# The first rows of a fused layer-norm, gated MLP and long-convolution training step: gate and up products of rows 0 and 1 advanced together, weight piece by weight piece

## The chip, the cores and the metric

The kernel runs on one core of a Trainium2 chip. The metric is the device time of one execution in microseconds. Before the change the median of three runs is 1850.38 us (1850.25 to 1850.51). Engines are named as in the profile: PE is the matrix engine, PEld its weight loads, DVE the vector engine, ACT the scalar engine, POOL the general engine and SP the engine that issues most of the transfers; "SPq" or "ACTq" marks an instruction of an engine's sequencer, such as a transfer being issued.

## The reference, cut to what matters

The program computes a forward pass and the gradients of all inputs. For this change only the forward's start matters: a layer norm of x, and two products of the normalised rows with weight matrices.

```python
def _layernorm(x, axis=-1, eps=1e-5):
    m = jnp.mean(x, axis=axis, keepdims=True)
    v = jnp.var(x, axis=axis, keepdims=True)
    return (x - m) / jnp.sqrt(v + eps)
...
        gate = jnp.einsum("bsd,df->bsf", x, W_gate)
        up = jnp.einsum("bsd,df->bsf", x, W_up)
        gate = gate * (lambda x, dt: x.astype(dt))(gate > 0, gate.dtype)
        h = gate * up
        return jnp.einsum("bsf,fd->bsd", h, W_down)
...
    xn = _layernorm(x, axis=-1)
    return x + _A_ref(xn, A_k, A_v, A_shift_k, A_ssm_k, A_ssm_D) + _B_ref(xn, B_W_gate, B_W_up, B_W_down)
```

x has 2048 rows of 1024 bfloat16 values; W_gate and W_up are 1024 by 3584, W_down is 3584 by 1024. The outputs are the result and nine gradients.

## The kernel before

Rows are taken in 16 tiles of 128 rows, columns of the MLP in 7 blocks of 512. `hidden` goes over two halves of eight row tiles, and in each over the seven blocks. For a row tile and a block it makes a gate product and an up product (eight matmuls each over the 1024 inner values, in `gemm8`, line 1111, into the PSUM tiles `ps_g` and `ps_u`), and a product of the incoming gradient tile with the transposed W_down block (`grad_row`, PSUM tile `ps_h`). [...]

A matmul needs the row tile with its inner index on the partitions. For tiles 0 to 5 `flip_xn` makes that on PE: eight 128 by 128 transposes into a PSUM tile `pst_x` (line 1154), then a copy to `xnT` (line 1159) by DVE, for tile 4 by ACT. Tiles 6 and 7 are turned by a transposing transfer.

The layer norm is a Python generator, `layer_norm`; each `next(ln)` emits one stage. Tile 0's mean and variance come from DVE's statistics instructions (line 1016); tile 1's from ACT, which sums a row of 1024 (line 962, `sums`) and then sums the squares after the mean is known. A row's reciprocal root comes from `root` and `inverse`: a few DVE instructions on one or two columns with one ACT square root between them. Tiles 0 and 1 are turned when they are only centred ("bare" rows): the factor `rstd` is put in later, in the relu on ACT (line 1230) and in the product with the mask on DVE (line 1244). Tile 2 and all later tiles are scaled before they are turned. `LN_CHUNKS` says how many tiles are loaded and normalised together: tiles 0 to 3 singly, from tile 4 on by pairs. A pair shares one root. `ln_load` loads a chunk into one of five buffers of four rows each, so the sixth load waits for the first buffer.

The order of the opening is written out by hand in `first_rows`: gate of row 0 (with the transposes of tile 1 after its sixth matmul), gate of row 1, up of row 0, up of row 1 (tile 2 turned after its fifth matmul), gate 2, up 2 (tile 3 turned after its fourth), gate 3, up 3. Before it, `warm` runs 42 small matmuls on zeros. After it come gradient rows 0 and 1; in row 1, after the fourth matmul, `flip_ahead` turns tiles 4 and 5. `chunk` emits stages of the layer norm behind the last ACT instruction of the layer norm.

A scheduler orders each engine's instructions by a priority that grows with the place in the program, and by when it expects their operands. An instruction given to `keep_in_program_order` (in the generator `hold`; through `pri.pin` with `always=True` elsewhere) keeps its place among those so marked. Engines then run their queues strictly in order. Transfers from SP share one queue: x tile 0 (half), the four pieces of the first W_gate block (256 KB each), four of W_up with the load of tile 2 in their middle, tile 3, four transposing loads of W_down with tiles 4 and 5 in their middle, gradient tiles 0 and 1 (transposing), tiles 6 and 7, gradient tiles 2 and 3. The second half of tile 0 and tile 1 are issued by ACT. Stores of the normalised rows go out from POOL: tile 0's at once, those of the other first-half tiles are kept in a list and sent in two groups.

Of the kernel before, what the change touches and what calls it, by code (L numbers as in the profile page):

```python
# [879 lines left out]
class LnMlp:  # L880
# [60 lines left out]
    def ln_load(self, x, xpool, i):  # L941
        if i >= len(self.LN_CHUNKS):
            return
        st0, n = sum(self.LN_CHUNKS[:i]), self.LN_CHUNKS[i]
        xt = xpool.tile([P, 4, self.D], BF16, name="ln_x", tag="lnx")
        rows = x[st0 * P:(st0 + n) * P, :].rearrange("(t p) d -> p t d", p=P)
        sy, ac, h = self.nc.sync, self.nc.scalar, self.D // 2
        parts = {0: ((sy, 0, h), (ac, h, self.D)), 1: ((ac, 0, self.D),)}.get(i, ((sy, 0, self.D),))
        for queue, lo, hi in parts:
            ins = queue.dma_start(out=xt[:, 0:n, lo:hi], in_=rows[:, :, lo:hi])  # L950
            if queue is ac:
                self.tc.keep_in_program_order(ins)
        self.ln_x.append(xt)

    def layer_norm(self, xn_d, jpool, jtag, spool):
# [19 lines left out]
        def root(sm, smb, n, pin, quarter):  # L975
            pin(V.tensor_scalar(out=smb[:, 2, 0:n], in0=smb[:, 1, 0:n], scalar1=LN_EPS, scalar2=None, op0=ALU.add))
            pin(act(sm[:, 4, 0:n], smb[:, 2, 0:n], ACT.Sqrt, scale=0.25))
            if quarter is None:
                pin(act(sm[:, 5, 0:n], smb[:, 2, 0:n], ACT.Copy, scale=0.25))
            else:  # L980
                quarter(V.tensor_scalar(out=sm[:, 5, 0:n], in0=smb[:, 2, 0:n], scalar1=0.25, scalar2=None, op0=ALU.mult))

        def inverse(sm, smb, n, st0, pin, amid=None):
            pin(V.reciprocal(out=sm[:, 6, 0:n], in_=sm[:, 4, 0:n]))
            if amid is not None:
                amid()
            if n == 1:
                ins = V.scalar_tensor_tensor(out=smb[:, 3, 0:n], in0=sm[:, 6, 0:n], scalar=sm[:, 5, 0:n],
                                             in1=sm[:, 4, 0:n], op0=ALU.mult, op1=ALU.add)
                if amid is not None:  # L990
                    pin(ins)
            else:
                V.tensor_tensor(out=sm[:, 5, 0:n], in0=sm[:, 5, 0:n], in1=sm[:, 6, 0:n], op=ALU.mult)
                V.tensor_tensor(out=smb[:, 3, 0:n], in0=sm[:, 4, 0:n], in1=sm[:, 5, 0:n], op=ALU.add)
            self.ln_dve = V.reciprocal(out=self.rstd[:, st0:st0 + n], in_=smb[:, 3, 0:n])
# [11 lines left out]

        h = D // 2
        x0, x1, c1 = self.ln_x[0][:, 0, :], self.ln_x[1][:, 0, :], self.ln_x[1][:, 1, :]
        (s0, b0), (s1, b1) = small(), small()  # L1010
        self.pri.now()

        def stats(x, smb):
            bn = spool.tile([P, 2, 6], F32, name="ln_bn")
            for k in range(2):
                hold(V.bn_stats(out=bn[:, k], in_=x[:, k * h:k * h + h]))  # L1016
                if k == 0:
                    yield
            hold(V.bn_aggr(out=smb[:, 0:2, 0], in_=bn[:].rearrange("p h s -> p (h s)")))

        for _ in stats(x0, b0):
            pass
        def less(c):
            hold(V.tensor_scalar(out=x0[:, c:c + h], in0=x0[:, c:c + h], scalar1=b0[:, 0, 0:1], scalar2=None,
                                 op0=ALU.subtract))

        hold(sums(s1[:, 0, 0:1], x1, ACT.Copy, scale=-1.0 / D))
        hold(act(b1[:, 0, 0:1], s1[:, 0, 0:1], ACT.Copy))
        root(s0, b0, 1, hold, None)
        less(0)  # L1030
        less(h)
        hold(sums(s1[:, 2, 0:1], x1, ACT.Square, bias=b1[:, 0, 0:1]))
        self.xn.append(x0)
        yield
        hold(V.tensor_scalar(out=c1, in0=x1, scalar1=b1[:, 0, 0:1], scalar2=None, op0=ALU.add))
        inverse(s0, b0, 1, 0, hold, lambda: None)
        hold(self.ln_dve)
        self.xn.append(c1)
        yield
        self.pri.now()  # L1040
        hold(V.tensor_scalar(out=b1[:, 1, 0:1], in0=s1[:, 2, 0:1], scalar1=1.0 / D, scalar2=None, op0=ALU.mult))
        root(s1, b1, 1, hold, hold)
        n0 = self.ln_x[0][:, 1, :]
        hold(V.tensor_scalar(out=n0, in0=x0, scalar1=self.rstd[:, 0:1], scalar2=None, op0=ALU.mult))
        nc.gpsimd.dma_start(out=xn_d[0:P, :], in_=n0)
        inverse(s1, b1, 1, 1, hold, lambda: None)
        hold(self.ln_dve)
        yield
        st0 = 2
        for i, n in list(enumerate(self.LN_CHUNKS))[2:]:  # L1050
# [3 lines left out]
            pin, d = hold if n == 1 else free, n // 2 * 2  # L1054

            def centre(j):
                return V.tensor_scalar(out=xt[:, d + j, :], in0=xt[:, j, :], scalar1=smb[:, 0, j:j + 1], scalar2=None,
                                       op0=ALU.subtract if i == 2 else ALU.add)
            if i == 2:
                yield from stats(xt[:, 0, :], smb)  # L1060
            else:
# [4 lines left out]
                if i == 4:  # L1066
                    yield
                ins = V.tensor_scalar(out=smb[:, 0, 0:n], in0=sm[:, 0, 0:n], scalar1=-1.0 / D, scalar2=None, op0=ALU.mult)
# [861 lines left out]
```

## Time and profile before

| what | value |
|---|---|
| median of three runs | 1850.38 us (1850.25 to 1850.51) |
| the profiled execution's own time | 1850.71 us |
| its span, first to last instruction | 1848.9 us |
| PE busy | 1829.2 us, 99% of the span |
| DVE busy | 1118.2 us, 60% |
| ACT busy | 643.9 us, 35% |
| share of the chain that ended last on PE | 98% |
| first transposes of tile 0 | 5.58 us |
| first matmul of gradient row 0 | 22.50 us |
| transposes of tiles 4 and 5 | from 25.15 us |

A line of the timeline gives the start, the length, the engine, the line of the program, the operation, the tile written and read, the shapes, how many were merged, and in brackets the idle time before it with what ended it. Matmuls are pipelined: one of 128 by 512 is listed with 0.38 us, but in a dense run they start 0.216 us apart. A line of the stretches gives the length of a stretch, the busy time and instruction count of each engine in it, the granted PE clock, the share of the transfer engines and the rate.

### The profile page before, as it was taken

What the parts mean: (1) busy time and instruction counts of PE and PEld (TensorE: products, weight loads), DVE (VectorE), ACT (ScalarE), POOL (GpSimd) and SP (SyncE); (2) the same over time, 40 slices, a digit from 0 to 9 for tenths busy, and PEclk for the clock granted to TensorE, in tenths of its full rate; (3) what the DMA queues carried; (4) which work ended last, traced back from release to release, by engine and by line L of the source; (5) the groups of instructions that cost most, each with busy time, mean ns of one, the idle gap of its engine ahead of it and who ended that gap; (6) DMA issues with size and microseconds to landing.
All of it is one profiled execution on the core that took longest, in us unless ns stands there. A gap on an engine that the chain in (4) does not pass through costs nothing.

```text
span 1848.9 us, 32175 instructions
## 1 busy us (share of the span) xinstructions
PE 1829.2 (99%) x12974; PEld 848.1 (46%) x13186; DVE 1118.2 (60%) x1649; ACT 643.9 (35%) x1209; POOL 34.8 (2%) x72
## 2 busy tenths in 40 slices
PE   9999999999999999999999999999999999999999
PEld 5444444444444444444444444444444544444444
DVE  6756898698789758585685667721122222566652
ACT  5644544545444454544544454320000000111100
POOL 2200000000000000000000000000000000000000
PEclk9999999999999999999999999999999999999999
DMA  9997669969767856639567445389999857799963
GB/s 259 282 224 177 156 169 235 217 161 205 187 152 205 240 159 162 169 103 270 130 158 170 142 117 160 106 243 251 219 233 266 198 143 172 171 211 214 208 148 74
DMA packets 746805, 345.18 MB, mean 187 GB/s; under 512 B 578088, under 2 KB 715296, under 8 KB 746656
## 3 DMA queue, kind: packets, MB, share of 16 engines
q1 hardware_dynamic: 732992, 311.39, 70.9%
q10 hardware_dynamic: 9504, 17.04, 3.0%
q0 software_dynamic: 4160, 14.68, 2.3%
q8 instruction: 103, 1.69, 0.4%
q14 instruction: 46, 0.38, 0.1%
HBM read 143.79 MB, written 103.83 MB: 134 GB/s over the span
## 4 chain that ended last, share of the span: by engine, by line
PE 98%; issue 1%; DVE 0%; ACT 0%; ACTq 0%
PE ps_x L1780 21%; PE ps_w L1483 20%; PE ps_h L1111 10%; PE ps_u L1111 10%; PE ps_o L1648 10%; PE ps_g L1111 10%; PE ps_d L1483 9%; PE ps_c L83 4%; PE ps_d L1499 1%; PE ps_w L1499 1%; PE ps_r L1682 0%; PE ps_warm L1170 0%; ACT ln_j L962 0%; PE pst_x L1154 0%; DVE ln_bn L1016 0%
## 5 line engine op out<-in xcount | busy, mean ns | idle before, releaser
L1483 PE MATMUL ps_w<-ugs,xn_nat 128*128 128x512 bf16 x1675 | 375.2, 379 | 4.7 <-issue 2.9
L87 ACT CAST arena<-ps_c 128x512 bf16<-128x512 f32 x576 | 293.8, 613 | 104.6 <-PE ps_c L83 104.3
L1111 PEld LDWEIGHTS <-xnT 128*128 128x128 bf16 x1792 | 171.8, 98 | 208.7 <-issue 5.1
L1483 PEld LDWEIGHTS <-xn_nat 128*128 128x128 bf16 x1728 | 165.3, 98 | 200.8 <-issue 6.1
L343 DVE STREAM_TRANSPOSE arena<-arena 128x1024 f32<-128x1024 f32 x96 | 179.4, 1934 | 112.2 <-ACT arena L87 101.8
L1111 PE MATMUL ps_u<-wu,xnT 128*128 128x512 bf16 x878 | 204.7, 379 | 1.2
L1111 PE MATMUL ps_g<-wg,xnT 128*128 128x512 bf16 x865 | 203.1, 379 | 1.5
L1111 PE MATMUL ps_h<-wdT,goT 128*128 128x512 bf16 x870 | 201.8, 379 | 1.3
L1780 PE MATMUL ps_x<-wuT,guT 128*128 128x512 bf16 x878 | 197.5, 379 | 1.0
L1780 PE MATMUL ps_x<-wgT,ggT 128*128 128x512 bf16 x878 | 197.3, 379 | 0.9
L1798 ACT ACTIVATE w<-xn,m 128x512 f32<-128x512 bf16 x32 | 24.3, 807 | 480.2 <-DVE m L1791 366.8
L1648 PE MATMUL ps_o<-wd,hT 128*128 128x512 bf16 (+1 forms) x879 | 186.7, 372 | 0.9
L1483 PE MATMUL ps_d<-g_nat,hs 128*128 128x512 bf16 x743 | 166.5, 379 | 2.6 <-issue 1.9
L1780 PEld LDWEIGHTS <-guT 128*128 128x128 bf16 x896 | 87.7, 98 | 105.7
L1780 PEld LDWEIGHTS <-ggT 128*128 128x128 bf16 x896 | 87.7, 98 | 105.5
L1111 PEld LDWEIGHTS <-goT 128*128 128x128 bf16 x896 | 86.6, 98 | 104.3 <-issue 1.0
L1648 PEld LDWEIGHTS <-hT 128*128 128x128 bf16 x896 | 87.7, 98 | 100.0
L1378 ACT CAST gh<-ps_h 128x512 bf16<-128x512 f32 x112 | 66.3, 592 | 190.6 <-PE ps_h L1111 181.7
L1486 ACT CAST wi<-ps_w 128x512 bf16<-128x512 f32 x108 | 64.5, 598 | 187.1 <-PE ps_w L1483 151.2
L1640 DVE TENSOR_TENSOR ya<-ya,xe 128x1024 bf16<-128x1024 bf16 x16 | 11.1, 692 | 182.1 <-DMA xe<-xn_d 182.1
L91 DVE TENSOR_TENSOR t<-arena 128x2048 bf16<-128x2048 bf16 x96 | 113.9, 1219 | 0.4
L1483 PEld LDWEIGHTS <-hs 128*128 128x128 bf16 x768 | 73.3, 98 | 88.3 <-issue 1.8
(150 smaller groups left out, 1412.8 us busy)
## 6 DMA issues: line engine op xcount, KB each, us to landing
ugs<-ug_d SPq DMA_DIRECT2D x112, 256.0 KB, 5.2
ug_d<-ru SPq DMA_DIRECT2D x104, 256.0 KB, 3.5
wg<-in_B_W_gate_dram SPq DMA_DIRECT2D x56, 256.0 KB, 4.9
wu<-in_B_W_up_dram SPq DMA_DIRECT2D x56, 256.0 KB, 4.3
hs<-h_d SPq DMA_DIRECT2D x56, 256.0 KB, 4.6
out_dram<-wi SPq DMA_DIRECT2D x56, 256.0 KB, 4.2
h_d<-ht SPq DMA_DIRECT2D x104, 128.0 KB, 2.2
gt<-in_grad_out_dram SPq DMA_DIRECT2D x32, 256.0 KB, 5.5
```

The costliest lines, as they stand in the source:

```text
L83: self.pri.pin(self.nc.tensor.matmul(out, lhsT=lhsT, rhs=rhs, start=start, stop=stop))
L87: self.pri.pin(self.nc.scalar.copy(out=out, in_=in_))
L91: self.pri.pin(self.nc.vector.tensor_tensor(out=out, in0=in0, in1=in1, op=op))
L343: self.pri.pin(self.nc.vector.transpose(out=df[:, c0:c0 + 32, :], in_=sf[:, c0:c0 + 32, :]))
L1111: self.pri.pin(self.nc.tensor.matmul(ps[:], lhsT=xT[:, kt * P:(kt + 1) * P], rhs=w(kt), start=(kt == 0), stop=(kt == self.DT - 1)), always ...
L1378: self.pri.pin(nc.scalar.copy(out=gh[:], in_=ps[:]))
L1483: self.pri.pin(self.nc.tensor.matmul(ps[:], lhsT=lhsT(st), rhs=rhs(st), start=(st == 0), stop=(st == self.ST - 1)))
L1486: self.pri.pin(self.nc.scalar.copy(out=out, in_=ps[:]))
L1499: self.pri.pin(self.nc.tensor.matmul(ps[i][:], lhsT=lhsT(i, st), rhs=rhs(i, st), start=(st == 0), stop=(st == self.ST - 1)))
L1648: nc.tensor.matmul(ps, lhsT=hT[:, kt, :], rhs=self.wd[:, kt, oc], start=(kt == 0), stop=(kt == self.FT - 1))
L1780: nc.tensor.matmul(ps, lhsT=T[:, kt, :], rhs=W[:, kt, oc], start=(i == 0), stop=(i == n - 1))
L1798: nc.scalar.activation(out=w[:, oc], in_=xn[:, oc], func=ACT.Identity, scale=m[:, 7:8], bias=m[:, 6:7])
```

## The change

- Loads: tile 1 moves from ACT's queue to SP's, the first W_gate piece from SP's to ACT's. The load of tile 2 is issued ahead of the second W_up piece, that of tile 3 ahead of the fourth. Tile 5 is no longer loaded with tile 4 but by itself, between gradient tiles 0 and 1 (`ln_rest`). The loads of the gradient tiles and of tiles 6 and 7 are pinned to program order.
- Layer norm: tile 0's mean comes half from a statistics instruction on DVE and half from an ACT sum (`half_mean`); its variance from an ACT square. Tiles 0 and 1 share one root. Tile 2 is also turned when only centred. Tile 3's mean is taken like tile 0's, and tiles 2 and 3 share one root. Tiles 4 and 5 keep one root for both, but each has its own stage of sums and squares.
- Order: 40 warm matmuls instead of 42. Tile 0 is transposed in pieces of 2, 2 and 4. `pair` writes two PSUM banks side by side: gate of row 0 takes weight piece 0, then tile 1 is turned, then pieces 1 and 2 for row 0, pieces 0, 1, 2 for row 1, piece 3 for both. The up rows alternate by weight piece; tile 2 is turned after the sixth pair of matmuls. The mask products of rows 0 and 1 on DVE come together, after tile 3 is turned.
- Stores: those of tiles 0, 1 and 2 are made from separate scaled copies and kept; the groups have four and four stores instead of three and four.

```diff
-        parts = {0: ((sy, 0, h), (ac, h, self.D)), 1: ((ac, 0, self.D),)}.get(i, ((sy, 0, self.D),))
+        parts = ((sy, 0, h), (ac, h, self.D)) if i == 0 else ((sy, 0, self.D),)
+        m = 1 if i == 4 else n
...
+        if i == 4:
+            self.ln_rest = lambda: sy.dma_start(out=xt[:, 1:2, :], in_=rows[:, 1:2, :])
...
+        def half_mean(x, s, b, k):
+            part = spool.tile([P, 2, 6], F32, name="ln_bn")
+            hold(V.bn_stats(out=part[:, 0], in_=x[:, 0:h]))
+            hold(sums(s[:, 0, k:k + 1], x[:, h:D], ACT.Copy, scale=-1.0 / D))
+            hold(V.tensor_tensor(out=s[:, 1, k:k + 1], in0=part[:, 0, 1:2], in1=part[:, 0, 4:5], op=ALU.add))
+            hold(V.scalar_tensor_tensor(out=b[:, 0, k:k + 1], in0=s[:, 1, k:k + 1], scalar=-0.25, in1=s[:, 0, k:k + 1],
+                                        op0=ALU.mult, op1=ALU.add))
...
+            if i == 4:
+                for j in range(n):
+                    hold(sums(sm[:, 0, j:j + 1], xt[:, j, :], ACT.Copy, scale=-1.0 / D))
+                    hold(act(smb[:, 0, j:j + 1], sm[:, 0, j:j + 1], ACT.Copy))
+                    hold(sums(sm[:, 2, j:j + 1], xt[:, j, :], ACT.Square, bias=smb[:, 0, j:j + 1]))
+                    moved(xt[:, n + j, :], xt[:, j, :], smb[:, 0, j:j + 1])
+                    yield
...
-        h = self.DT // 2 if st < 3 else self.DT
-        for k0 in range(0, self.DT, h):
+        k1 = 0
+        for h in {0: (2, 2, 4), 1: (4, 4)}.get(st, (8,)):
+            k0, k1 = k1, k1 + h
...
-        return st < 2
+        return st < 3
...
+                ps = pair("ps_g", wg, ((0, 0), (0, 1), (0, 2), (1, 0), (1, 1), (1, 2), (0, 3), (1, 3)), {0: second_tile})
+                for s in range(2):
+                    gate(s, True, ps=ps[s])
+                    yield from step()
                 next(ln)
...
+                ps = pair("ps_u", wu, [(s, q) for q in range(4) for s in range(2)], {5: third_tile})
+                for s in range(2):
+                    up(s, None, {}, lambda *fs: held.extend(fs), True, ps[s])
+                    yield from step()
+                gate(2, True)
                 yield from step()
                 up(2, None, {3: last_mid})
                 chunk(1)
                 yield from step()
                 gate(3, True)
+                chunk(1)
                 yield from step()
                 up(3, hold=True)
+                chunk(1)
                 yield from step()
...
-                self.warm(42)
+                self.warm(40)
...
-                        for put in self.kept[0:3] if sp == 2 else self.kept[3:7]:
+                        for put in self.kept[0:4] if sp == 2 else self.kept[4:8]:
...
+    first = [b.col_block(B_W_gate, 0, "wg", 0, ahead=tc.nc.scalar)]
     b.first_root()
-    first = [b.col_block(B_W_gate, 0, "wg", 0)]
-    first.append(b.col_block(B_W_up, 0, "wu", 1, lambda: load(2)))
-    load(3)
+    first.append(b.col_block(B_W_up, 0, "wu", 1, {1: lambda: load(2), 3: lambda: load(3)}))
     first.append(b.row_block_T(B_W_down, 0, "wdT", 2, lambda: load(4)))
-    goT = [b.load_T(g, i, "goT", 8 + i) for i in range(2)]
+    goT = [b.load_T(g, 0, "goT", 8, True)]
+    b.ln_rest()
+    goT.append(b.load_T(g, 1, "goT", 9, True))
     load(5)
-    goT += [b.load_T(g, i, "goT", 8 + i) for i in range(2, 4)]
+    goT += [b.load_T(g, i, "goT", 8 + i, True) for i in range(2, 4)]
```

More of the change, by code (lines that the diff above doesn't have):

```diff
@@ L1011, in layer_norm @@
+        c0, c1, n1, n0 = self.ln_x[0][:, 1, :], *(self.ln_x[1][:, k, :] for k in (1, 2, 3))
+        c2, n2 = (self.ln_x[2][:, k, :] for k in (1, 2))
+        (sm, smb), (s2, b2) = small(), small()
         self.pri.now()
[L1013 to L1019, printed above, removed]
@@ L1042, in layer_norm @@
[L1042 to L1047, printed above, removed]
-        yield
-        st0 = 2
-        for i, n in list(enumerate(self.LN_CHUNKS))[2:]:
+        variance(sm, smb, 2, hold)
+        root(sm, smb, 2, hold)
+        inverse(sm, smb, 2, 0, held)
```

198 lines of the change are left out of this document (97 added, 101 removed).

## The prediction

> **What bounds the kernel now.** I read the page first: how busy the matrix engine (PE) is, and the chain that ended last.
>
> ```profile
> span 1848.9 us, 32175 instructions
> PE 1829.2 (99%) x12974; PEld 848.1 (46%) x13186; DVE 1118.2 (60%) x1649; ACT 643.9 (35%) x1209; POOL 34.8 (2%) x72
> PE 98%; issue 1%; DVE 0%; ACT 0%; ACTq 0%
> ```
>
> PE is the bound, and the chain leaves other engines under 2% of the span. The change touches only the opening, so I read that as busy time by stretch, next.
>
> ```profile
> core 0: us, PE busy (x) PEld busy (x) DVE busy (x) ACT busy (x) POOL busy (x), PEclk, DMA share, GB/s
> 5.50:10.60 5.10, 5.05 (x34) 2.73 (x33) 4.16 (x19) 3.45 (x9) 0.32 (x1) 1.00 1.07 357
> 10.60:22.50 11.90, 11.57 (x65) 5.42 (x65) 10.39 (x32) 8.61 (x16) 0.94 (x2) 1.00 1.12 226
> 22.50:26.30 3.80, 3.75 (x30) 2.11 (x30) 3.49 (x13) 1.80 (x5) 1.07 (x2) 1.00 1.08 252
> 26.30:60.00 33.70, 33.54 (x154) 15.23 (x157) 21.77 (x67) 17.86 (x31) 16.10 (x26) 1.00 1.11 271
> ```
>
> PE is idle by only 0.05, 0.33 and 0.05 us up to 26.3 us, and VectorE (DVE) is nearly as full (10.39 of 11.90 us). So what can be won is about one microsecond in 1850; what can be lost is whatever wait the new order makes. Last I read the timeline of the opening for the rows that decide it.
>
> ```profile
> 1.02 4.66 PE L1170 MATMUL ps_warm<-warm 128*128 128x128 bf16 x42 [1.02 <-DVE warm L1167]
> 5.58 1.03 PE L1154 MATMUL pst_x<-ident,ln_x 128*128 128x128 bf16 x8
> 12.42 0.58 SPq L950 DMA_DIRECT2D ln_x<-in_A_q_dram  x1
> 13.84 0.62 PE L1154 MATMUL pst_x<-ident,ln_x 128*128 128x128 bf16 x8 [0.26 <-DVE ln_x L998]
> 17.58 2.66 SPq L1135 DMA_TRANSPOSE goT<-in_grad_out_dram  x2
> 17.73 1.06 ACT L962 ACTIVATE ln_j<-ln_x 128x1024 bf16<-128x1024 bf16 x1 [0.26 <-DMA ln_x<-in_A_q_dram]
> 20.43 0.44 SPq L950 DMA_DIRECT2D ln_x<-in_A_q_dram  x1
> 21.31 1.13 ACT L962 ACTIVATE ln_j<-ln_x,ln_b 128x1024 bf16<-128x1024 bf16 x1
> 22.57 0.17 DVE L1076 TENSOR_SCALAR ln_b<-ln_s 128x2 bf16<-128x2 f32 x1 [0.53 <-ACT ln_j L962]
> 24.51 0.97 DVE L998 TENSOR_SCALAR ln_x<-ln_x,rstd 128x1024 bf16<-128x1024 bf16 x2
> 25.15 1.07 PE L1154 MATMUL pst_x<-ident,ln_x 128*128 128x128 bf16 x16
> ```
>
> See two places. At 13.84 us tile 2's transposes waited for its full normalisation; start to start that gap is 0.63 us where the pitch is 0.216, so 0.42 us is lost (the other visible gap, at 18.63, loses 0.18). At 25.15 us the transposes of tiles 4 and 5 start right behind a chain: load (issued at 12.42), two sums and two squares on ScalarE (ACT), roots, scaling. That chain and PE finish together today; PE loses 0.06 us there.
>
> **The change, part by part.** Starts are those of single instructions in the timeline; landings are the last semaphore update of a transfer.
>
> *Start.* Two warm matmuls go: 2 x 0.107 us. Tile 0's mean takes one half by DVE statistics (0.70) and one by an ACT sum (1 element 0.19, 1024 elements 1.06, so about 0.62 for 512), then 0.16 and 0.22 on DVE, in place of two statistics, an aggregate (0.21) and an addition. The halves landed at 3.51 and 3.70, so the first centred half is done near 5.07 (before: 5.52). PE ends its 40 warm matmuls at 5.27 and starts there, 0.31 us earlier than 5.58. Eight transposes at 0.107 end at 6.12; the copy of the first two (0.29) ends at 6.02, so the first gate matmul starts at 6.12 (before 6.57).
>
> *Tile 1 is turned after two gate matmuls instead of six.* These end near 6.9. Centring of tile 1 needs its load, an ACT sum and mean (5.77 to 7.16 today) and 0.49 us of DVE. Today tile 1's load landed at 5.75 and the transposes could have begun at 7.73; PE came at 7.96, so nobody waited. The load moves to the SP queue and weight piece 0 takes its place on ACT's. If tile 1 lands by 5.2, DVE's copies of tile 0 set it (centring 6.71 to 7.19, turn at 7.25); if as today, 7.73. I take the middle, 7.5: PE idles 0.6 us (ends 0.35 and 0.85) where it did not. Then 8 transposes at 0.056 and 14 matmuls at 0.216 end at 10.97 (10.7 to 11.2); before, 10.60. Landings of weight pieces (6.74, 7.49, 8.23) are all earlier than their matmuls.
>
> *From the up rows to the first gradient row*: 48 matmuls x 0.216 + 16 transposes x 0.056 = 11.26 us, against 11.90 before. Tile 2's turn no longer needs the root (centred near 12.3, wanted at 13.5); up pieces 1 and 3 move back one place each behind the loads of tiles 2 and 3 (from 9.72 to about 10.4, from 11.88 to 12.6, wanted 11.9 and 14.0); tile 3's centring, joint root and scaling end near 16.9, wanted at 17.4. Each is covered, the last by only 0.5 us. Rows 0 and 1, and 2 and 3, share one root: about ten small DVE operations of 0.15 to 0.22 go, tile 3's half statistics and row 2's flag (0.70 and 0.28) come; DVE is about 1 us lighter. The first gradient row would start at 22.2 (22.0 to 22.5; before 22.50). After 12 matmuls (2.59) PE wants tile 4 at 24.8, 0.35 us earlier than now.
>
> *Stores and pins.* Tile 0's store leaves POOL at 10.28 (0.71) and goes to the group at 43 us, where POOL issues four (0.65 each) instead of three, behind nothing on PE: nothing. If that cover went, a later load into the buffer would wait 0.65. It also frees 256 KB of transfer at 13.5 to 14.5 us (0.7 us). The pins on the gradient tiles and on the load of tiles 6 and 7 keep today's order; gradient tile 2 landed at 26.86, wanted at 33.99: nothing.
>
> *Tiles 4 and 5, the term that decides.* One load of 512 KB issued at 12.42 becomes 256 KB there (tile 4) and 256 KB behind gradient tile 0 (tile 5). Its two ACT phases can't end before the second half lands, and the root is joint for both rows. Today: landing 17.65, squares end 22.53, transposes 25.15. When does the second half land? SP's second transposed load behind a plain one stays in issue until that one lands (14.33 to 17.54 behind 17.65; 22.20 to 25.25 behind 25.36). With half the bytes and no store beside it, tile 4 lands near 16.3; gradient tile 0 is then issued 16.3 to 17.6, the new load at 17.7. A plain load amid transposed ones lands late: the one for tiles 6 and 7 landed 5.1 us after the issue ahead of it ended (20.24 to 25.36) for 512 KB, so some 4.1 for half: 21.7. By bytes alone (gradient tile 0's landing 21.41, less 1.4 saved by the store and the smaller load, plus 0.72) it is 20.7; with nothing saved before it, 18.89 + 4.1 = 23.0. I take 21.5, nearest to the like load. From there ACT needs a sum with mean 1.3 and a square 1.25: squares end at 24.1 instead of 22.53. Behind them on ACT's in-order queue waits row 3's relu, and for it row 3's mask and product on DVE. From the squares to the transposes took 2.6 us, some 0.5 of it behind two products: 2.1 alone, or 2.95 if row 3's mask and product (0.66 + 0.34), now traced ahead of the inverse, run first. So tile 4 is turned at 26.2 to 27.05, against 25.15: **1.05 to 1.9 us later**; I take 1.5. The 0.35 us that PE came earlier is spent waiting. With 20.7 the least is +0.25, with 23.0 the most +3.4. Behind 26 us no row shows idle PE to win it back.
>
> The sum: span 1848.9 + 1.5 = 1850.4. The profiled execution took 1850.71 against a median of 1850.38, so its 1852.2 is 1851.9 beside the median.
>
> [...]
>
> **The rivals.** *The second half is in time.* If SP runs further ahead than I think and it lands by about 19.5, squares end at 22.1 and PE takes tile 4 when it comes, at 24.6 to 25.1: 0 to 0.6 us won, 1849.9 likely (1849.6 to 1850.4). For it: SP issued transposes in 1.3 us when unblocked, DMA has idle stretches near 12 us. Against: no plain load issued between transposes landed in under 4 us.
>
> *The wait stretches*: the h_d stores that POOL starts at 21.7, now some 2 us earlier, share the DMA with the new load and it lands past 23, while DVE runs all its products first: +3.4 to +4, 1854.1.
>
> *The clock falls (the far side, slower by over 0.2%).* PE would idle from 24.8 to 26.7 in one piece, longer than any gap now (0.63). If that lost the full clock, the opening shows the price: transposes cost 1.03 us for eight, later 0.61, and the slow state lasted from 1.02 to 6.6 us; 5.6 us at half pace cost 2.8. With the wait, +4.3 to +5: 1855. It decides from the length of idleness at which the clock is taken back, which no gap here shows. [...]
>
> **How the numbers follow.** Forecast 62% (its own range 1850.6 to 1853.7), in time 26%, stretched 6%, clock 6%. Time 1851.9. The range leaves out the clock, half of the stretched case and few of the in-time one: 1849.7 to 1853.7. A measurement here can tell about 0.2%, or 3.7 us, from no change: 1846.7 to 1854.1. No case gains that; the clock and a little of the stretched case lose it: faster 0.01, same 0.92, slower 0.07.
>
> **What would show it.** Right: first transposes near 5.27 and a PE gap before tile 1's near 7.5; no gap at tile 2's; the first gradient row at 22.0 to 22.5; then one gap of 1.5 to 2 us before tile 4's transposes, ended by DVE's scaling, with ACT waiting for tile 5's load until near 21.5. Wrong: that load landed before 20, a gap elsewhere above 0.5 us (tile 3's, or the second gradient row waiting for its tile, which lands behind the new load at about 23.2, wanted at 23.9), or the pitch back at 0.43 us behind the gap.

## The result, and the profile after

The changed kernel takes 1855.25 us, the median of 22 runs (1852.82 to 1857.05), against 1850.43 us for the kernel before on the same chip (22 runs, 1849.91 to 1851.07). The ratio is 1.0024, with a 95% interval of 1.0017 to 1.0031. The forecast was 1851.9 us with a range up to 1853.7, so the change costs 4.8 us where I had expected 1.5.

The profiled execution of the changed kernel took 1854.18 us, and its granted clock was 1.00 from 6.06 us, where its clock records begin, to the end of the span. First its page: the span, the busy time of each engine, and the shares of the chain that ended last.

```profile
span 1852.0 us, 32391 instructions
PE 1843.9 (100%) x13184; PEld 848.3 (46%) x13184; DVE 1119.3 (60%) x1651; ACT 646.3 (35%) x1212; POOL 34.9 (2%) x72
PE 96%; DVE 1%; SPq 1%; DMA 1%; issue 0%; ACT 0%; DVEq 0%
```

The span is 3.1 us longer, and SP's queue, a DMA and DVE have come into the chain that ended last, which was PE and little else before. PE's busy time can't be compared: the page of before counts 12974 matmuls and this one 13184, because records are missing there. Next, busy time by stretch of the changed kernel, at the same edges as before (the first figure after the stretch is its length, then busy time and instructions of each engine).

```profile
5.50:10.60 5.10, 4.62 (x32) 2.52 (x31) 3.67 (x14) 3.60 (x9) 0.00 (x0) 1.00 1.05 362
10.60:22.50 11.90, 11.90 (x68) 5.80 (x67) 10.47 (x32) 7.57 (x15) 1.31 (x2) 1.00 1.10 202
22.50:26.30 3.80, 2.17 (x11) 0.78 (x8) 3.08 (x12) 2.57 (x6) 0.88 (x2) 1.00 1.05 320
26.30:60.00 33.70, 32.78 (x163) 15.28 (x164) 20.17 (x64) 16.65 (x27) 15.23 (x26) 1.00 1.01 254
```

PE idles 0.48 us in the first stretch (0.05 before), nothing in the second (0.33 before), and 1.63 + 0.92 us in the last two, where it idled 0.05 + 0.16. The rows of the changed kernel's timeline behind this (start, duration, engine, line, operation, and in brackets the idle time ahead and what ended it):

```profile
5.26 0.99 PE L1163 MATMUL pst_x<-ident,ln_x 128*128 128x128 bf16 x8
7.17 0.62 PE L1163 MATMUL pst_x<-ident,ln_x 128*128 128x128 bf16 x8 [0.48 <-DVE ln_x L1009]
10.65 2.75 PE L1286 MATMUL ps_u<-wu,xnT 128*128 128x512 bf16 x12
13.24 0.61 PE L1163 MATMUL pst_x<-ident,ln_x 128*128 128x128 bf16 x8
17.71 0.58 SPq L955 DMA_DIRECT2D ln_x<-in_A_q_dram  x1
21.33 1.06 ACT L965 ACTIVATE ln_j<-ln_x 128x1024 bf16<-128x1024 bf16 x1 [1.44 <-DMA ln_x<-in_A_q_dram]
21.91 2.75 PE L1119 MATMUL ps_h<-wdT,goT 128*128 128x512 bf16 x12
24.02 0.17 DVE L1012 TENSOR_SCALAR ln_b<-ln_s 128x2 bf16<-128x2 f32 x1 [0.46 <-ACT ln_j L965]
24.52 0.69 DVE L1258 SCALAR_TENSOR_TENSOR ru<-ru,ps_u 128x512 bf16<-128x512 bf16 x1
25.25 0.42 DVE L1264 TENSOR_TENSOR ht<-ru 128x512 bf16<-128x512 bf16 x1
25.85 0.68 DVE L1399 TENSOR_TENSOR ru<-ru,gh 128x1024 bf16<-128x1024 bf16 x1
26.64 1.14 DVE L998 TENSOR_SCALAR ln_x<-ln_x,rstd 128x1024 bf16<-128x1024 bf16 x2
27.19 1.27 PE L1163 MATMUL pst_x<-ident,ln_x 128*128 128x128 bf16 x16 [2.52 <-DVE ln_x L998]
```

Down to 21.91 us this is the opening that was forecast, and the first gradient row starts 0.58 us earlier than before. Then tile 5's own load (L955), issued at 17.71 us, holds back ACT until 21.33 (1.44 us idle); row 3's relu, whose gate product PE had ended at 20.35, stands behind the squares in ACT's queue and starts at 23.90; the squares end at 23.99; DVE starts the variance at 24.02 and puts three operations that are not the normalisation's (L1258, L1264, L1399) ahead of the scaling; PE waits 2.52 us and turns tile 4 at 27.19 us instead of 25.15.

A second, smaller loss stands where no step of mine looked, near 247 to 250 us, inside one of the blocks of the first half. Before:

```profile
247.28 0.41 PE L83 MATMUL ps_c<-arena,RB 64*32 64x512 bf16 x7 [0.18 <-DVE ru L1247]
```

and after, with DVE's work ahead of it:

```profile
246.40 0.29 DVE L1243 TENSOR_SCALAR ru<-ru 128x512 bf16<-128x512 bf16 x1
246.79 0.75 DVE L1255 SCALAR_TENSOR_TENSOR ru<-ps_u,rstd,ru 128x512 bf16<-128x512 f32 x1
249.25 0.68 DVE L1258 SCALAR_TENSOR_TENSOR ru<-ru,ps_u 128x512 bf16<-128x512 bf16 x1
249.97 0.41 PE L83 MATMUL ps_c<-arena,RB 64*32 64x512 bf16 x7 [0.63 <-DVE ru L1258]
```

Tile 2 was turned while only centred, and so its row carries a flag (0.29 us) and a product with the factor (0.75 us instead of 0.68) in each of the seven blocks of the first half. At this one place DVE sets the time, and PE waits 0.45 us longer for row 3's mask.

To see where the span grows I paired the 4976 matmuls into ps_c, which both kernels have, one by one. The first of them, at 122 us, starts 2.24 us later than before; behind 250 us it is 2.69; at 541 us another 0.1 is lost, and at 853 us a wait for a DMA adds 0.31. These last two are left out of the sum below, because they stand in some profiles and not in others: at 853 us e5 loses 0.25 us and e6 1.3, while e1, e3, e4 and e7 lose nothing there. Around the span lie 2.2 us, where the execution of before had 1.8.

These terms explain only the quicker runs. The 22 runs are of two kinds by their recorded granted clock: 8 have 1.000 (median 1853.39 us), 14 have 0.999 or 0.998 (median 1855.69). All runs of before have 1.000. For the first kind 2.24 + 0.45 + 0.35 = 3.04 us stands against a measured 1853.39 - 1850.43 = 2.96. The other 2.3 us, in two runs of three, come with a lower clock; the experiments look for where it is lost.

### The profile page after: what moved, and what is told of

Read it like the earlier page. It is cut to its first block, busy times and chain, and to the rows that moved or that the text cites. A ratio compares the mean times of both kernels' runs of the same rounds, so it can differ in the third digit from the quotient of the medians.

```text
span 1852.0 us, 32391 instructions
## 1 busy us (share of the span) xinstructions
PE 1843.9 (100%) x13184; PEld 848.3 (46%) x13184; DVE 1119.3 (60%) x1651; ACT 646.3 (35%) x1212; POOL 34.9 (2%) x72
## 4 chain that ended last, share of the span: by engine, by line
PE 96%; DVE 1%; SPq 1%; DMA 1%; issue 0%; ACT 0%; DVEq 0%
PE ps_x L1800 21%; PE ps_w L1503 20%; PE ps_o L1668 10%; PE ps_g L1119 10%; PE ps_u L1119 10%; PE ps_h L1119 10%; PE ps_d L1503 9%; PE ps_c L83 4%; PE ps_d L1519 2%; SPq L1137 0%; PE ps_r L1702 0%; PE ps_w L1519 0%; DMA xn_nat<-xn_d 0%; DVE arena L343 0%; DMA wg<-in_B_W_gate_dram 0%
## 5 line engine op out<-in xcount | busy, mean ns | idle before, releaser
L1503 PE MATMUL ps_w<-ugs,xn_nat 128*128 128x512 bf16 x1728 | 381.1, 379 | 0.0
```

What stands on the lines that cost most here:

```text
L1503: self.pri.pin(self.nc.tensor.matmul(ps[:], lhsT=lhsT(st), rhs=rhs(st), start=(st == 0), stop=(st == self.ST - 1)))
```

## The experiments

Each median is over all runs of its kernel. "Full clock" counts the runs with a recorded granted clock of 1.000. The kernel before, on the same chips, was at 1850.29 to 1850.86 us.

| run | median (range) | ratio, 95% interval | full clock | PE idle before tile 4 in the profile, us |
|---|---|---|---|---|
| after | 1855.25 (1852.82 to 1857.05) | 1.0024, 1.0017 to 1.0031 | 8 of 22 | 2.52 |
| e1_whole | 1853.27 (1852.69 to 1854.80) | 1.0016, 1.0007 to 1.0025 | 8 of 11 | 2.12 |
| e2_late5 | 1854.85 (1853.04 to 1856.52) | 1.0023, 1.0014 to 1.0032 | 3 of 11 | 3.28 |
| e3_fill | 1854.16 (1853.00 to 1855.13) | 1.0019, 1.0010 to 1.0027 | 11 of 11 | 0.45 |
| e4_again | 1855.51 (1853.02 to 1858.64) | 1.0027, 1.0018 to 1.0035 | 4 of 11 | 2.79 |
| e5_tail | 1852.79 (1851.88 to 1854.21) | 1.0012, 1.0003 to 1.0021 | 11 of 11 | 1.42 |
| e6_noflag | 1854.10 (1852.08 to 1855.63) | 1.0018, 1.0009 to 1.0027 | 4 of 11 | 2.07 |
| e7_early | 1851.22 (1850.22 to 1853.76) | 1.0005, 0.9996 to 1.0014 | 10 of 11 | none |
| e8_turned | 1859.71 (1858.32 to 1860.63) | 1.0050, 1.0036 to 1.0064 | 0 of 5 | none |
| e9_turnlate | 1860.82 (1858.46 to 1864.16) | 1.0057, 1.0043 to 1.0070 | 0 of 5 | none |
| e10_behind | 1859.93 (1855.45 to 1861.01) | 1.0046, 1.0032 to 1.0059 | 1 of 5 | none |

### Is it the late load? Tile 5 put back beside tile 4

```diff
-        m = 1 if i == 4 else n
+        m = n
         ...
-            self.ln_rest = lambda: sy.dma_start(out=xt[:, 1:2, :], in_=rows[:, 1:2, :])
+            self.ln_rest = lambda: None
```

> The changed kernel with one thing undone: tile 5 is loaded together with tile 4, as before (no load between gradient tiles 0 and 1). Theory: the late load makes PE wait 2.9 us before the transposes of tiles 4 and 5, and that long gap also costs the full clock in most executions. Then here ACT's second sum starts right behind the first square, the squares end near 22.6 instead of 24.0, tile 4 is turned near 25.8, the gap shrinks to about 1.4 us, the granted clock is 1.000 in all runs and the median is about 1851.3 (1850.6 to 1852). Rival A: the lost clock comes from the opening itself (two warm matmuls fewer, and the 0.86 us gap before tile 1's transposes), which stays here: then some runs keep a clock of 0.999 and the median stays above 1853. Rival B: the time is lost by the extra flag of row 2 and other work outside the opening: then it stays near 1854 with the clock at 1.000.

The load of both tiles now landed at 18.05 us instead of 21.31, but PE's wait shrank by 0.4 us only. Pieces of the chain of waits of this run (start, duration, what):

```profile
11.81 6.24 DMA ln_x<-in_A_q_dram
...
18.13 1.16 ACT ln_j L965 x2
...
19.55 0.49 DVE ln_x L1009
...
24.15 0.69 DVE ru L1258
24.84 0.08 DVE ln_s L988
24.92 0.38 DVE ht L1264
25.30 0.08 DVE ln_s L993
...
25.57 0.60 DVE ru L1399
26.17 0.09 DVE rstd L995
...
26.28 0.50 DVE ln_x L998
26.82 0.62 PE pst_x L1163 x8
```

The squares ended at 23.34 us, only 0.65 us earlier than with the late load. A load still heads this chain, but its data are there at 18.05 us, and what follows takes the time: ACT works on the two tiles' sums and squares without a break from 18.13 to 23.34 us, and DVE runs one operation behind the other from 19.55 on. The same three operations of DVE still came between root and scaling, so tile 4 was turned at 26.82 us, a good microsecond after what I had expected. So taking the late landing away uncovers ACT's and DVE's own work, which ends almost as late. By its clock (3 of 11 runs lower) and its median (1853.27 us) this run came out as rival A had it, that the clock is lost in the first 8 us; the filled run and e4 below decide against that.

### The late load alone, put into the kernel before

```diff
-            ins = queue.dma_start(out=xt[:, 0:n, lo:hi], in_=rows[:, :, lo:hi])
+            m = 1 if i == 4 else n
+            ins = queue.dma_start(out=xt[:, 0:m, lo:hi], in_=rows[:, 0:m, lo:hi])
...
+            self.ln_rest = lambda: sy.dma_start(out=xt[:, 1:2, :], in_=rows[:, 1:2, :])
...
-    goT = [b.load_T(g, i, "goT", 8 + i) for i in range(2)]
+    goT = [b.load_T(g, 0, "goT", 8)]
+    b.ln_rest()
+    goT.append(b.load_T(g, 1, "goT", 9))
```

> The kernel before with one part of the change alone: tile 5 is loaded by itself between gradient tiles 0 and 1. Theory: the second sum waits for that load (about 21.5 to 22.5), both squares follow it, tile 4 is turned at about 27.5 to 28.5 instead of 25.15, PE gap 2.6 to 3.6 us, and part of the runs lose the clock: median 1853 to 1856, with runs at two levels some 2 us apart. Rival A (the clock is lost by the new opening's first 8 us): 1853 with the clock at 1.000 in all runs. Rival B (the late load is harmless): 1850.4.

```profile
28.81 1.19 PE L1157 MATMUL pst_x<-ident,ln_x 128*128 128x128 bf16 x16 [3.28 <-DVE ln_x L1001]
```

In the old order the same load costs more: tile 4 is turned at 28.81 us after 3.28 us of waiting, and the first ps_c matmul comes 5.34 us later than before in the profiled execution, 1.7 us of them, by the estimate below, from the clock. The late load is enough to lose the time by itself; with the rest of the change the wait was shorter in the profiles.

### The clock: the same wait filled, and the same kernel again

```diff
             def flip_ahead(sp):
+                if sp == 0:
+                    ps = self.ps_tile("ps_fill")
+                    for _ in range(11):
+                        self.pri.pin(nc.tensor.matmul(ps[:], lhsT=self.ident[:], rhs=wg(0), start=True, stop=True),
+                                     always=True)
```

> The changed kernel with 11 more 512-column matmuls (2.4 us), whose result nobody reads, put on PE between the fourth matmul of gradient row 1 and the transposes of tile 4, where PE waits 2.9 us. They take the place of idle time only, so the wait stays and the idleness goes. Theory: the clock is lost through this idle gap; with it filled all runs have a clock of 1.000 and the median is 1852.8 to 1853.5, the level of the changed kernel's runs with a full clock. Rival A (clock lost in the first 8 us): as the changed kernel, 1855.2 with most runs at 0.999. Rival C (the whole of the slowdown is the wait itself): also 1855.2, with a clock of 1.000.

> The changed kernel once more, on the chip of the other three. Theory: two kinds of runs, 1852.8 to 1854.4 with a clock of 1.000 and 1855.0 to 1857 with 0.999 or less, the second kind in more than half; if its profile falls on the second kind, the timeline shows matmuls at a pitch of 0.43 us somewhere between 27 and 35 us. Rival A: the slow pitch stands between 6 and 12 us. Rival D: no slow pitch anywhere in the opening, the clock is lost elsewhere in the program.

The filling matmuls compute nothing that is used. PE's rows of the filled run:

```profile
24.58 2.54 PE L1392 MATMUL ps_fill<-wg,ident 128*128 128x512 bf16 x10
27.56 1.27 PE L1163 MATMUL pst_x<-ident,ln_x 128*128 128x128 bf16 x16 [0.45 <-DVE ln_x L998]
```

Tile 4 comes no earlier (27.56 us), so nothing about the wait's cause has changed, yet none of 11 runs lost the clock, where 7 of 11 did for the changed kernel itself on the same chip. The median of the filled kernel, 1854.16 us, is above the 1852.8 to 1853.5 that I had expected. It lies 0.1 us above the four full-clock runs of e4 on the same chip (median 1854.06) and 0.8 above those of after on another; in its profile tile 4 comes 0.37 us later than in after, and near 143 us an up row waits for its weights and 0.6 us more is lost. The profile of e4, the changed kernel once more, caught the loss. Its windows (stretch, length, busy time and count of each engine, then the granted clock, DMA share and rate):

```profile
24.90:28.32 3.42, 0.82 (x12) 0.65 (x13) 3.10 (x9) 0.69 (x3) 1.24 (x2) 1.00 1.40 231
28.32:31.73 3.41, 3.19 (x14) 1.55 (x13) 1.10 (x3) 3.41 (x7) 0.00 (x0) 0.50 0.99 290
31.73:35.14 3.41, 3.41 (x17) 1.57 (x16) 2.15 (x9) 3.28 (x7) 0.68 (x1) 1.00 1.22 328
```

The three stretches are cut at the trace's clock records: full from 4.42 us, half from 28.317 to 31.730, full again. 28.317 is 4.423 + 7 x 3.413 us, and the loss lasts 3.413 us; e2's fall at 29.614 us is 7 such steps behind its first full clock at 5.721. In both traces, then, the clock changed a whole number of 3.413 us steps after it was first full, and the step with 2.6 us of idle PE was followed by one that ran wholly at half clock. From these records I estimate the cost of 3.41 us at half clock at 1.7 us; in the five rows of the table above with at least three runs of each kind (after, e1, e2, e4 and e6), the median of the lower kind lies 1.55 (e2) to 2.3 us (after) above that of the full kind. What makes it more than 1.7 in after is not shown. Cutting every profile into windows of 3.413 us from its first full clock (its grid) gives PE's idle time in the window with most of it, leaving out the first and the last 10 us of the program:

| run | idle of 3.41 us | the next window |
|---|---|---|
| e3_fill | 0.3 | full |
| e7_early | 0.7 | full |
| e6_noflag | 1.1 | full |
| e5_tail | 1.5 | full |
| e1_whole | 1.5 | full |
| after, the profiled run | 1.9 | full |
| e10_behind | 2.6 | half |
| e4_again | 2.6 | half |
| e2_late5 | 2.6 | half |
| e9_turnlate | 2.9 | half, and the one after it |
| e8_turned | 3.4 | half, and the one after it |

The window with the most idle time in the profiled run of after, against the lost one above, is

```profile
23.12:26.54 3.42, 1.55 (x8) 0.49 (x5) 2.86 (x12) 1.99 (x5) 1.08 (x2) 1.00 1.05 320
```

Here the same wait was cut by the grid's edge at 26.54 us, so no window held more than 1.87 us of it. The grid's phase differs from execution to execution (the first full clock came at 3.8 us in e5, at 6.06 in after and at 6.9 in e3), which in my reading would explain that one kernel has both kinds of runs. In the profiles of the table a window at full clock with up to 1.9 us of idleness was followed by full clock, and one with 2.6 us or more by half. A rival reading is that the transposes of a tile do not count as work; then the lost windows of e2 and e4, in which PE does nothing else (0.80 and 0.82 us busy), would have been wholly idle. It does not fit: e10 lost the clock with 0.86 us of ordinary matmuls in the window, and e1 kept it with 0.66 us of them beside its transposes. Behind a lost window less idle time went with a further one: the first window at half clock held 1.6 us of idle time in e8 and 2.0 us in e9 and was followed by another at half clock, while that of e4, with 0.2 us, was followed by full clock.

One profile does not tell what the other executions of its kernel waited. The opening of e6 below is the changed kernel's, operation for operation, and its late load landed a microsecond earlier than in after:

```profile
20.32 1.06 ACT L965 ACTIVATE ln_j<-ln_x 128x1024 bf16<-128x1024 bf16 x1 [0.98 <-DMA ln_x<-in_A_q_dram]
```

The same load landed at 21.31 us in after, 21.59 in e4, 21.68 in e3 and 21.55 in e5. So e6's wait of 2.07 us is that of one early execution, and its 7 lower runs of 11 agree with the 21 of 33 of the changed kernel. One count stays unexplained: one run of e7 lost the clock, and its profile, of another run, has no gap of over 1.0 us.

### DVE's order: all of tiles 4 and 5's normalisation ahead of row 3's product

```diff
                 gate(3, True)
-                chunk(1)
+                chunk(2)
                 yield from step()
                 up(3, hold=True)
-                chunk(1)
                 yield from step()
```

> The changed kernel, late load of tile 5 kept, but both last stages of tiles 4 and 5 (variance and root, then inverse and scaling) stand ahead of the third up product, so that row 3's mask and product and gradient row 0's product no longer run on DVE between the root and the scaling. Theory (after the run with tiles 4 and 5 loaded together, whose gap was still 2.5 us): the three foreign DVE operations, 1.8 us in all, are a part of the wait as large as the late load. Squares end near 24.0 as now, tile 4 is turned near 26.0 instead of 27.19, the PE gap falls from 2.9 to about 1.7 us, the clock is 1.000 in all runs, median 1852.2 (1851.7 to 1852.8). Rival (the load alone sets it): tile 4 stays near 27, median 1855 with most runs at 0.999.

DVE's rows of this run, from the squares on:

```profile
24.26 0.17 DVE L1012 TENSOR_SCALAR ln_b<-ln_s 128x2 bf16<-128x2 f32 x1 [0.45 <-ACT ln_j L965]
...
25.50 0.17 DVE L995 RECIPROCAL rstd<-ln_b 128x2 f32<-128x2 bf16 x1
25.70 0.88 DVE L998 TENSOR_SCALAR ln_x<-ln_x,rstd 128x1024 bf16<-128x1024 bf16 x2
26.50 0.68 DVE L1258 SCALAR_TENSOR_TENSOR ru<-ru,ps_u 128x512 bf16<-128x512 bf16 x1
```

From variance to scaling it takes 1.44 us where the changed kernel takes 2.62, and row 3's mask now follows. From the end of the squares to the first transpose of tile 4 it takes 2.02 us; with the order of the changed kernel it took 3.2 in all four profiles that have it (after, e3, e4, e6), whenever the load landed. Tile 4 is turned at 26.25 us, 0.94 earlier; the first ps_c matmul is 1.10 us later than before instead of 2.24; and with PE's wait at 1.42 us in the profile the clock fell in none of 11 runs. Against the full-clock runs of after the medians differ by 0.6 us only, less than the trace's 1.1, with runs 2 us apart; the full-clock medians of after and e4, one and the same kernel, lie 0.67 us apart.

### The bare row 2 in blocks 1 to 6

```diff
                 def masked():
-                    if self.bare(s0 + s):
+                    if self.bare(s0 + s) and not (n and s == 2):
```

This kernel leaves out row 2's factor (the reciprocal root) in the masked product of blocks 1 to 6, with its flag.

> The changed kernel in which row tile 2, in blocks 1 to 6 of the first half, takes the mask form of the scaled rows: no flag instruction (0.28 us) and a mask product of 0.68 instead of 0.74 us. This leaves the factor rstd out of that row's up product in those six blocks. Theory: keeping tile 2 unscaled costs DVE 0.35 us in every block, and in the one block where DVE sets PE's pace (around 249 us) PE waits 1.01 us instead of 0.56; here that gap is back at 0.56, everything ahead of it as in the changed kernel, and the runs with a full clock lie at 1852.9 instead of 1853.4 (median still mixed, about 1855). Rival: the gap at 249 us has another cause (the later start of the other branch) and stays at 1.0.

The place near 249 us is back at the time of before:

```profile
248.51 0.41 PE L83 MATMUL ps_c<-arena,RB 64*32 64x512 bf16 x7 [0.17 <-DVE ru L1258]
```

The gaps of 1.01 and 0.56 us named above run from start to start; the brackets give the idle time alone. The wait of 0.63 us is 0.17, as before (0.18), and the lag behind the kernel before does not grow there (1.24 us ahead of the place, 1.22 behind it). So the recurring flag and factor are the 0.45 us. The whole times do not resolve it: the four full-clock runs have a median of 1852.64 us, 0.75 under those of after, but 0.35 of this lies around the span, and the opening was early in the profile.

### A version without the wait

```diff
-        m = 1 if i == 4 else n
+        m = n
...
-    first.append(b.row_block_T(B_W_down, 0, "wdT", 2, lambda: load(4)))
+    load(4)
+    first.append(b.row_block_T(B_W_down, 0, "wdT", 2, lambda: None))
...
-                gate(2, True)
+                gate(2, True, {5: lambda: chunk(1)})
...
-                ps = pair("ps_g", wg, ((0, 0), (0, 1), (0, 2), (1, 0), ...), {0: second_tile})
+                ps = pair("ps_g", wg, ((0, 0), (0, 1), (0, 2), (1, 0), ...), {1: second_tile})
...
-        kept(n1, c1, 1)
-        kept(n2, c2, 2)
...
+            if i == 4:
+                kept(n1, c1, 1)
+                kept(n2, c2, 2)
```

Both tiles are loaded ahead of W_down's first pieces, their stages stand earlier, the scaled copies of tiles 1 and 2 come behind their scaling, and tile 1 is turned behind two weight pieces.

> An arrangement meant to keep the gains and drop the wait: tiles 4 and 5 are loaded together and ahead of all transposing loads; tile 4's sums start before row 2's relu and tile 5's before row 3's; their scaling stands ahead of the scaled copies of tiles 1 and 2 and of row 3's mask and product; tile 1 is turned after weight pieces 0 and 1 of row 0 instead of after piece 0. Theory: tiles 4 and 5 land near 14, squares end near 21.5, tile 4 is scaled at 24.0 to 24.4 when PE asks for it (24.1 to 24.3), so the gap is under 0.3 us, the gap at 6.3 us shrinks by 0.4, no run loses the clock. Against the changed kernel PE is 2.9 us earlier behind tile 5's transposes; the 0.45 us at 249 us and the 0.35 us outside the span stay: median 1850.3 (1849.9 to 1850.8). If another wait takes the place (weights of W_down, now later by one load), the gap is before the first gradient row.

```profile
24.19 1.06 PE L1163 MATMUL pst_x<-ident,ln_x 128*128 128x128 bf16 x16
...
246.76 0.41 PE L83 MATMUL ps_c<-arena,RB 64*32 64x512 bf16 x7 [0.63 <-DVE ru L1258]
```

PE turns tile 4 without waiting at 24.19 us, 0.96 earlier than before, and is 0.97 us ahead at 122 us; at 246.76 it gives 0.45 of that back to the bare row 2. The span of this execution is 1848.4 us against 1848.9, but over all runs the median span is 1849.1 us against 1848.7, and 2.1 us lie around it against 1.8. The median of 1851.22 us is above the 1849.9 to 1850.8 that I had expected, and one run of 11 lost the clock. The ratio, 1.0005 (0.9996 to 1.0014), can't be told from no change. So without its wait the change shows no gain here.

### Turning tiles 0 to 2 again, scaled

To end the recurring cost, the three bare tiles were turned once more from their scaled copies, by three transposing loads, and blocks 1 to 6 ran without flag and factor.

```diff
+                if ahead and sp == 2:
+                    for s in range(3):
+                        xT[s] = self.act_tile("xnT", s)
+                        self.tc.keep_in_program_order(nc.sync.dma_start_transpose(
+                            out=xT[s][:].rearrange("p (a b) -> p a b", b=P), in_=self.scaled[s]))
...
-                kw = dict(scale=self.rstd[:, s:s + 1]) if self.bare(s0 + s) else {}
+                kw = dict(scale=self.rstd[:, s:s + 1]) if ahead and self.bare(s0 + s) else {}
```

> As the arrangement before it, and tiles 0, 1 and 2 are turned once more, from their scaled copies, by three transposing transfers around 40 us, so that from block 1 on no row is unscaled: no flags and no factors for rows 0 to 2 in blocks 1 to 6. Theory: DVE is lighter by about 1 us in each of these blocks; the gap near 249 us falls from 1.0 us to 0.1 or less, the rest is unchanged, so it is 0.6 to 0.9 us faster than that arrangement: median 1849.5 (1849.1 to 1849.9), below the kernel before. Rival: DVE does not set the pace there, no difference.

SP's queue, and the waits of PE between 40 and 60 us (in total, times, longest):

```profile
37.57 8.51 SPq L1461 DMA_TRANSPOSE xnT<-ln_x  x3
46.13 5.26 SPq L1145 DMA_TRANSPOSE goT<-in_grad_out_dram  x2
```

```profile
PE ps_h L1121 <- DMA goT<-in_grad_out_dram: 6.7, 1, 6.7
```

Gradient tiles 6 and 7, pushed behind the turns on SP, came 6.7 us late, and two windows of half clock followed (51.93 to 58.75 us). The place near 249 us did end as a loss: the lag to the kernel before fell there by 0.55 us. The next run was to move the turns behind these two tiles.

> The early kernel with tiles 0 to 2 turned again from their scaled copies, the three turning loads now issued behind those of gradient tiles 6 and 7 instead of ahead of them. My theory: the 7 us gap at 46 us came from these two gradient tiles being pushed behind the turns on SP, so here it is gone and the clock stays full; with no flag and no rstd factor on bare rows in blocks 1 to 6 the gap of about 1.0 us near 246 us is gone too, so the span is about 0.4 to 0.5 us under the early kernel's 1848.37: 1847.6 to 1848.1, and the median, with 1.8 to 2.15 us outside the span, 1849.7 to 1850.8, against 1851.22. The rival: the three turns cost on the DMA queue wherever they stand, so a gap of over 1 us shows between 46 and 80 us and the median is 1851.5 or more.

Its edit caught a second line with the same condition and moved gradient rows 4 and 5 as well, so its gaps, up to 4.0 us at 61 us, can't be put down to the turns. The next one moves the turns alone:

```diff
-                if ahead and sp == 2:
+                if ahead and sp == 4:
                     for s in range(3):
```

> The kernel of the late turn with one thing put right: that run also moved the gradient rows 4 and 5 from the second pair's place to the third's, which I had not meant, so its gaps at 36 us (the gradient rows cut short by gate matmuls) and at 61 us (before gradient rows) can't be put down to the turns alone. Here only the three turning loads move, behind those of gradient tiles 6 and 7. If the moved gradient rows made those gaps, none over 1 us shows behind 20 us, the gap near 246 us is gone, the span is 1847.6 to 1848.3 and the median 1849.7 to 1850.8. If the turns cost on the DMA queue wherever they stand, a gap of over 1 us is left between 46 and 80 us, before what is loaded behind them (up weights or W_down), and the median is 1851.5 or more.

SP's queue and PE's waits between 35 and 80 us in this run:

```profile
42.06 8.89 SPq L1461 DMA_TRANSPOSE xnT<-ln_x  x3
51.04 2.23 SPq L1113 DMA_DIRECT2D wu<-in_B_W_up_dram  x4
53.37 9.50 SPq L1139 DMA_TRANSPOSE wdT<-in_B_W_down_dram  x4
```

```profile
PE ps_h L1121 <- DMA wdT<-in_B_W_down_dram: 2.5, 1, 2.5
PE ps_u L1121 <- DMA wu<-in_B_W_up_dram: 1.8, 2, 1.6
```

The three turns hold SP for 8.89 us. Up weights, issued at 42.12 us in e7, start at 51.04, and W_down behind them; PE waits for both, and the window behind the second wait (63.12 to 66.54 us) runs at half clock. My theory for this place fell: in e7 the queue has no free 9 us between 34 and 57 us, so the turns delay what stands behind them in both places that were tried. Issuing them in a later block was not tried.

## Why the prediction was wrong, and where it was right

Two steps failed: the wait before tile 4 was sized too small, and the loss of the clock that this wait brought in 21 of 33 runs was given 6% and left out of the range. Two smaller costs, outside the opening and around the span, were put at nothing.

**Start** held: the first transposes at 5.26 us (forecast 5.27). **Tile 1 turned after two gate matmuls** held in kind, and was better in size: tile 1 landed at 5.07 us, the early branch of my working (by 5.2), and was turned at 7.17 instead of 7.5, PE waiting 0.48 us instead of 0.6, the up rows starting at 10.65 instead of 10.97. **From the up rows to the first gradient row** held: no wait at tile 2 (13.24) or tile 3, and the first gradient row at 21.91, just below the 22.0 to 22.5 given.

**Stores and pins**, costed at nothing, showed no wait of PE in the first 60 us.

**Tiles 4 and 5, the term that decides**, named the right mechanism and the right place. The late half landed at 21.31 us (21.5 forecast) and the squares ended at 23.99 (24.1). It was mis-sized behind that: from the squares to the transposes I gave 2.1 to 2.95 us, with row 3's mask and product as the most that could come between, and took a value amid the two. It took 3.2, in four profiles alike: both of these came between, and a third operation, gradient row 0's product (0.68 us, L1399, at 25.85 us), stood ahead of the scaling too. My upper end was also added up wrong: 2.1 + 0.66 + 0.34 is 3.10, not 2.95. That this sum would have come within 0.1 of the 3.2 is luck, for it has two operations and three ran; the three together cost 1.18 us (3.20 against e5's 2.02). So tile 4 came 2.04 us later, not 1.5 (at most 1.9 by that landing), and tile 5's transposes waited 0.20 more, which I had not counted. e5 shows the order of DVE's work as the part that could be had back.

**"DVE is about 1 us lighter"** counted row 2's flag once. The flag and factor recur in every block of the first half, and at one place, near 249 us, DVE has no slack: 0.45 us, shown by e6. My sentence that "behind 26 us no row shows idle PE" looked for time to win back and not for a place where DVE was already the limit; the 0.18 us wait of before at 247.28 was such a row.

**The sum** took what lies around the span, 1.8 us, as fixed. It is 2.1 to 2.25 us in after, e1, e3, e4, e5 and e7, and 1.7 to 1.85 in before, e2, e6, e8, e9 and e10. Why is open; e6, which differs from after in one line of blocks 1 to 6, has 1.8.

**The rival "the clock falls"** got 6% and happened in 21 of the 33 runs of the changed kernel (14 of 22, and 7 of 11 in e4). I had named the deciding quantity, the length of idleness, and then took what is needed to lie above my own estimate of 1.9 us of waiting; that was not shown, since the trace of before, whose longest gap there is 0.63 us, can't show it. In the runs up to 1.9 us of idle time in one window kept the clock (after) and 2.6 us lost it (e2, e4, e10), and the wait was 2.07 to 2.79 in the three profiles of this opening (after, e4, e6). Even with the wait sized right the rival would still have looked unlikely to me; an unknown limit near the forecast wait deserved far more than 6%. That this rival's 1855 us lies so near the measured 1855.25 is partly luck: it had 1.5 us for the wait and 2.8 for the clock, and the runs showed 2.96 in all at full clock and 1.55 to 2.3 for the clock.

Put together for the full-clock runs: 1850.43 + 2.04 + 0.20 + 0.45 + 0.35 = 1853.47 us, measured 1853.39. So close a fit is partly luck, since e4's full-clock runs of the same kernel have a median of 1854.06 and the load's landing moved by over a microsecond between executions. The runs with a lower clock, two in three, lie another 2.3 us higher, of which one lost window explains 1.7, and the median lands among these.

**The rival "in time"** (26%) is out: the load landed 3.6 us behind the issue ahead of it, near the 4.1 that I took from a like load. But its premise, that an earlier landing brings tile 4 in time, is out as well: in e1 the data were there at 18.05 us and PE still waited 2.12 us.

## What to carry to other kernels

Where a change makes PE wait, price the clock too: in this kernel 2.6 us of waiting inside one window of 3.41 us cost a further 1.7 us, by the estimate above (medians 1.55 to 2.3 us apart), in some executions and not in others, and 1.9 us did not. Shorten such a wait or fill it: with 1.42 us (e5) and 0.45 us (e3) of waiting left, none of 11 runs each lost the clock. When a late input moves a chain, list every operation that stands between its steps on the same engine: here three of DVE's ahead of the scaling cost 1.18 us. And an operation saved once in the opening is not a saving if it is paid again in every block: look for the one place where that engine already sets the time.

## What the runs showed of the hardware that I had not expected

- The granted clock fell 7 steps of 3.413 us after it was first full in both e4 and e2. A window of that length with 2.6 us of idle PE (e2, e4, e10) was followed by half the clock for the whole next one; one with 1.9 us (after) was not. 3.4 us (e8) and 2.9 us (e9), with another 1.6 and 2.0 us idle in the next window, were followed by two windows at half clock (6.83 us).
- Three transposing loads of 256 KB from on-chip buffers held SP's queue for 8.5 (e8) and 8.9 us (e10), while the two of the same size ahead of them in e10 held it for 2.7. Why the three take longer is open.
- The time around the span was about 2.15 us in after, e1, e3, e4, e5 and e7 and about 1.8 us in before, e2, e6, e8, e9 and e10, for kernels that do nearly the same work. In the trace the updates up to 1.71 us after the last instruction agree in both; the last four come from 1.81 to 1.93 us in before and from 2.20 to 2.32 in after.
